# A mixing layer's second product packed from twelve matmuls a block to eleven, with whole token blocks transposed

## The chip, the cores and the metric

The kernel runs on one core of a Trainium2 chip. The metric is the device time of one execution in microseconds, as the median of several runs. A core has TensorE (PE in the profile, its weight loads PEld), VectorE (DVE), ScalarE (ACT), GpSimd (POOL) and SyncE (SP), whose queue (SPq) issues all DMAs of this kernel.

## The reference

x has 2048 tokens of 448 numbers. After a layernorm, a two-dimensional Fourier filter and a mixer work on the same input, and both results are added to x:

```python
x = A_x
xn = _layernorm(x, axis=-1)
return x + _A_ref(xn, A_w_r, A_w_i) + _B_ref(xn, B_w1, B_w2, B_w3, B_w4)
```

The change is in the first half of the mixer:

```python
h = _gelu(_layernorm(x, axis=-1) @ w1)
c = D // 4
g0 = jnp.pad(h[:, :, 0*c:1*c], ((0, 0), (1, 0), (0, 0)))[:, :S, :]   # shift +1
g1 = jnp.pad(h[:, :, 1*c:2*c], ((0, 0), (0, 1), (0, 0)))[:, 1:, :]   # shift -1
g2 = jnp.pad(h[:, :, 2*c:3*c], ((0, 0), (2, 0), (0, 0)))[:, :S, :]   # shift +2
g3 = jnp.pad(h[:, :, 3*c:   ], ((0, 0), (0, 2), (0, 0)))[:, 2:, :]   # shift -2
hs = jnp.concatenate([g0, g1, g2, g3], axis=-1) @ w2
x1 = x + hs
h2 = _gelu(_layernorm(x1, axis=-1) @ w3) @ w4
return x1 + h2
```

So each quarter of h (112 columns) is moved by one or two tokens up or down, and the product with w2 (448 x 448) mixes the quarters. w3 is 448 x 1792, w4 is 1792 x 448.

## The kernel before

**Blocks.** Token a*16 + b stands in partition a of block b, so there are 16 blocks of 128 tokens. A shift by tokens takes a quarter from another block, and only where it wraps around (blocks 0, 1, 14 and 15) does the partition change by one. The blocks are worked in groups of four: 14, 15, 0, 1; then 2 to 5; 6 to 9; 10 to 13.

**Precision.** All large products are in 16 bits with each operand as a high and a low half: high x high, high x low and low x high are added up in PSUM (PASS). ScalarE makes the high half and VectorE or POOL the low one (split_w, and the last operations of w1_unit and ln2). Weights are scaled by a power of two found from the sum of their squares (squares, powers).

**Stages.** warm_up first keeps TensorE busy with matmuls on zeros (line 817). norm1 normalizes a group in place; its refine() on POOL makes the exact scales, among them gsc, which the gelu uses. T1 transposes a group on TensorE (line 374), and the halves go to xT (378, 379). w1_in is the first product (line 414). w1_unit applies the gelu (433), writes the halves of h for one block to a buffer hs of 2 x 4 quarters, each of 112 columns padded to 128 (434, 435), and one DMA transpose of 8 x 128 columns (438) takes it to hT, where the tokens lie along the columns. w2_tile (line 454) makes a block of the second product with 4 quarters x 3 passes = 12 matmuls on 112 rows each, the quarter k taken from the block at distance SHIFT[k], at a column offset for the wrap; it then adds x (456). ln2 is the second layernorm; its transposes (490) go to x2all. turn() transposes the fourth group by DMA (842). front (line 385) and back (line 787) are the products with w3 and w4. Further on come the Fourier stages and the rest of the second mixer product.

**Order.** Each engine works its own queue in order. A scheduler sets the order from the program's priorities and from its own estimates; behind(...) fixes that one operation is issued after another. While TensorE's queue has products of several stages, the pieces of a block of w2_tile can stand between them.

**Memory.** x2mem holds x2all; its later part first holds w4 as it is loaded (w4raw, four loads from line 228, issued behind the transposes of the second and third group), so x2all's groups from the second on have to wait for w4's split.

Of the kernel before, what the change touches and what calls it, by code (L numbers as in the profile page):

```python
# [12 lines left out]
F32 = mybir.dt.float32  # L13
# [7 lines left out]
NB, NC = 16, 16  # L21
# [4 lines left out]
SHIFT = [1, -1, 2, -2]  # L26
WARM = 28
# [9 lines left out]
HS = 3  # L37
# [31 lines left out]
def constants():  # L69
# [20 lines left out]
    for c in range(NC):  # L90
        for j8, (k1, t) in enumerate(slots(c)):
            for j, (kr, s, base) in enumerate(rows(c)):
                if base != k1:
                    continue
                phi = tau * np.outer(np.arange(NB), kr + 128 * np.arange(16)) / S
# [28 lines left out]
def body(tc, nc, x, wf, w1, w2, w3, w4, c_g, c_n, c_small, out):  # L124
# [46 lines left out]

    def stage(name, n, side, dtype=F32):
        t = pw.tile([128, 1808], F32, tag=f"stage{side}", bufs=1, name=name)
        return (t if dtype is F32 else t.bitcast(dtype))[:, :n]
# [19 lines left out]
    def load_x(g):  # L194
        for b0 in sorted(GRP[g])[::2]:
            SY.dma_start(xt[b0 // 2], xv[:, b0:b0 + 2])
# [9 lines left out]
    SY.dma_start(w2s[:112], w2.rearrange("(k p) n -> p k n", p=112))  # L206
# [14 lines left out]
    x2mem = pw.tile([128, 9 * F], F16, name="x2mem")  # L221
    x2all = x2mem[:, 0:8 * F].rearrange("p (j t n) -> p j t n", j=4, t=7)
    w4raw = x2mem.bitcast(F32)[:, F:].rearrange("p (f n) -> p f n", f=14)
    w4v = w4.rearrange("(f p) n -> p f n", p=128)
    W4F = (0, 4, 8, 11, 14)

    def load_w4(i):
        SY.dma_start(w4raw[:, W4F[i]:W4F[i + 1]], w4v[:, W4F[i]:W4F[i + 1]])

    csm = pc.tile([128, 2 * (256 + 2 * DF + 452 + 128)], F16, name="csm")  # L230
# [162 lines left out]
    w2p = pr.tile([112, 2, 4, D], F16, name="w2p")  # L393
# [3 lines left out]

    def h_alloc(g):
        t = {0: 0, 1: 1, 2: 2, 3: 1}[g]
        hT[g] = pr.tile([128, 8, 512 if g else 592], F16, tag=f"h{t}", name=f"h{g}")  # L400
        if g == 0:
            P.memset(hT[g][:, :, 0:576].rearrange("p t (b a) -> p t b a", b=4)[:, :, :, 0:16], 0.0)
            P.memset(hT[g][:, :, 576:592], 0.0)

    def h_at(g, i):
        return 128 * i if g else 144 * i + 16
# [9 lines left out]

    hs_buf = [p1.tile([128, 2, 4, 128], F16, name=f"hs{i}") for i in range(HS)]
    for t in hs_buf:
        P.memset(t.rearrange("p i k n -> p (i k) n")[:, :, 112:], 0.0)

    for o in (0, 1024):
        hs_buf.append(x2mem[:, o:o + 1024].rearrange("p (i k n) -> p i k n", i=2, k=4))
        P.memset(hs_buf[-1].rearrange("p i k n -> p (i k) n")[:, :, 112:], 0.0)

    def w1_unit(g, i, pm=None):
        if pm is None:
# [4 lines left out]
        pv_ = pm.rearrange("p (k n) -> p k n", k=4)  # L431
        h = hs_buf[c % (HS if g == 3 else HS + 2)]
        A.activation(out=pm, in_=pm, func=AF.Gelu_apprx_tanh, scale=gsc[:, c:c + 1])
        u = A.activation(out=h[:, 0, :, 0:112], in_=pv_, func=AF.Copy, scale=h1)
        v = V.scalar_tensor_tensor(out=h[:, 1, :, 0:112], in0=pv_, scalar=h1, in1=h[:, 0, :, 0:112],
                                   op0=ALU.mult, op1=ALU.subtract)
        o = h_at(g, i)
        d = SY.dma_start_transpose(out=hT[g][:, :, o:o + 128], in_=h.rearrange("p i k n -> p (i k n)"))
        after[g, i] = u.ins, v.ins
        after["h", g, i] = (d.ins,)  # L440

    def w2_tile(b):
        pm = bank("sp", f"pw2_{b}")
        n = 0
        for k in (2, 0, 1, 3):
            src, o = b - SHIFT[k], 1
            if src < 0:
                src, o = src + NB, 0
            elif src >= NB:
                src, o = src - NB, 2  # L450
            g, i = WHERE[src]
            o += h_at(g, i) - 1
            for hi, wi in ((0, 0), (0, 1), (1, 0)):
                T.matmul(pm[:, :D], hT[g][:112, 4 * hi + k, o:o + 128], w2p[:, wi, k], start=n == 0, stop=n == 11)  # L454
                n += 1
# [311 lines left out]
    def back(G, fp):  # L767
# [10 lines left out]
        for i in range(2):  # L778
# [12 lines left out]
            if end:  # L791
                with prio(EVAC):
                    for r, to in parts:
                        V.scalar_tensor_tensor(out=xb(b)[:, r], in0=to, scalar=p34[:, min(G, 1):min(G, 1) + 1],  # L794
                                               in1=xb(b)[:, r], op0=ALU.mult, op1=ALU.add)
                        if G > 4:
                            SY.dma_start(ov[:, b, r], xb(b)[:, r])
# [271 lines left out]
```

## Time and profile before

| | |
|---|---|
| median of 3 runs | 410.89 us (410.64 to 411.07) |
| the profiled execution | 410.65 us, span 408.9 us |
| TensorE busy | 402.3 us, 98% of the span |
| VectorE, ScalarE, POOL busy | 330.7, 256.5 and 95.3 us |
| TensorE's granted clock | 1.00 |

A row of the chain of waits or of the timeline begins with its start and its length in us. In a row of groups the number behind x is a count, then come the busy time in us and the mean of one in ns. A row of windows gives for one stretch the busy time of PE, PEld, DVE, ACT and POOL, then the clock, the DMA share and GB/s. A row of DMA issues ends with the median time from issue to landing. L numbers are lines of the kernel.

### The profile page before, as it was taken

What the parts mean: (1) busy time and instruction counts of PE and PEld (TensorE: products, weight loads), DVE (VectorE), ACT (ScalarE), POOL (GpSimd) and SP (SyncE); (2) the same over time, 40 slices, a digit from 0 to 9 for tenths busy, and PEclk for the clock granted to TensorE, in tenths of its full rate; (3) what the DMA queues carried; (4) which work ended last, traced back from release to release, by engine and by line L of the source; (5) the groups of instructions that cost most, each with busy time, mean ns of one, the idle gap of its engine ahead of it and who ended that gap; (6) DMA issues with size and microseconds to landing.
All of it is one profiled execution on the core that took longest, in us unless ns stands there. A gap on an engine that the chain in (4) does not pass through costs nothing.

```text
span 408.9 us, 8745 instructions
## 1 busy us (share of the span) xinstructions
PE 402.3 (98%) x3409; PEld 299.0 (73%) x3409; DVE 330.7 (81%) x686; ACT 256.5 (63%) x434; POOL 95.3 (23%) x172
## 2 busy tenths in 40 slices
PE   7999999999999999999999999999999999999996
PEld 3655555765668777777887887877777779998995
DVE  4888999898857678887798888955899989966645
ACT  4698879973758866556598888863453554453431
POOL 3877720101336748400012111110000000000000
PEclk9999999999999999999999999999999999999999
DMA  8959879914786456516255666500011022100101
GB/s 278 354 192 179 153 149 321 177 62 90 156 231 202 137 196 210 170 59 183 63 145 143 155 156 171 147 27 3 24 68 69 25 88 85 55 2 2 45 2 45
DMA packets 56168, 51.28 MB, mean 125 GB/s; under 512 B 37632, under 2 KB 50496, under 8 KB 56128
## 3 DMA queue, kind: packets, MB, share of 16 engines
q1 hardware_dynamic: 56128, 50.74, 46.0%
q8 instruction: 26, 0.43, 0.4%
q14 instruction: 14, 0.11, 0.1%
HBM read 38.28 MB, written 3.67 MB: 103 GB/s over the span
## 4 chain that ended last, share of the span: by engine, by line
PE 94%; DVE 3%; DMA 2%; POOL 0%; issue 0%; ACT 0%; SPq 0%; POOLq 0%
PE pw L385 33%; PE acc L787 23%; PE pw L454 9%; PE pw L414 6%; PE side L757 4%; PE acc L757 3%; PE pu L646 3%; PE ps L543 3%; PE pe L667 2%; PE pp L601 2%; PE px L618 2%; PE py L688 2%; DVE sta L293 1%; DMA xt<-x 1%; DMA h<-hs 1%; PE pta L374 1%
## 5 line engine op out<-in xcount | busy, mean ns | idle before, releaser
L385 PE MATMUL pw<-x2mem,w3p 128*128 128x256 f16 x1232 | 151.1, 273 | 0.0
L385 PEld LDWEIGHTS <-w3p 128*128 128x128 f16 x1232 | 119.2, 98 | 20.6
L787 PE MATMUL acc<-w4p,hf 128*128 128x448 f16 (+1 forms) x516 | 105.4, 348 | 0.0
L787 PEld LDWEIGHTS <-hf 128*128 128x128 f16 x516 | 49.8, 98 | 36.5
L705 ACT ACTIVATE pw<-pw,pe 128x512 f32<-128x512 f32 x42 | 27.5, 655 | 35.7 <-PE pw L385 35.7
L708 DVE SCALAR_TENSOR_TENSOR hf<-pw,h,hf 128x512 f16<-128x512 f32 x42 | 31.3, 748 | 14.5 <-ACT hf L707 14.4
L454 PE MATMUL pw<-w2p,h 112*128 112x448 f16 x192 | 39.9, 352 | 0.8 <-DMA h<-hs 0.8
L414 PE MATMUL pw<-w1p,xT 128*128 128x448 f16 x176 | 35.4, 352 | 0.0
L627 POOL TENSOR_TENSOR z<-te 128x450 f32<-128x450 f32 x16 | 15.7, 982 | 70.3 <-DVE te L625 70.3
L454 PEld LDWEIGHTS <-h 112*128 112x128 f16 x192 | 18.6, 98 | 17.2 <-DMA h<-hs 1.0
L707 ACT ACTIVATE hf<-pw,h 128x512 f16<-128x512 f32 x42 | 28.7, 686 | 1.0
L414 PEld LDWEIGHTS <-xT 128*128 128x128 f16 x176 | 16.9, 98 | 16.4 <-DVE xT L379 0.8
L723 ACT ACTIVATE hz<-g,h 128x896 f16<-128x896 f32 x14 | 14.6, 1044 | 22.3 <-DVE g L720 22.2
L757 PEld LDWEIGHTS <-hz 128*128 128x128 f16 x294 | 28.2, 98 | 0.4
L608 ACT ACTIVATE pf<-pp 64x450 f16<-64x450 f32 x32 | 17.4, 544 | 12.3 <-DVE pf L609 8.0
L609 DVE TENSOR_TENSOR pf<-pp,pf 64x450 f16<-64x450 f32 x32 | 19.9, 622 | 3.4 <-ACT pf L608 3.0
L724 DVE SCALAR_TENSOR_TENSOR hz<-g,h,hz 128x896 f16<-128x896 f32 x14 | 16.1, 1150 | 7.6 <-ACT hz L723 7.6
L623 ACT ACTIVATE te<-px 64x450 f32<-64x450 f32 x32 | 17.3, 542 | 1.2 <-PE px L618 0.6
L526 POOL TENSOR_TENSOR f<-xr 128x452 f32<-128x452 f32 x16 | 16.4, 1046 | 0.6
L717 ACT ACTIVATE g<-pw,pe 128x512 f32<-128x512 f32 x14 | 9.6, 684 | 10.2 <-PE pw L385 10.1
L794 DVE SCALAR_TENSOR_TENSOR xt<-acc,p,xt 128x448 f32<-128x448 f32 (+1 forms) x17 | 10.9, 654 | 6.2 <-PE acc L787 6.0
L523 POOL TENSOR_TENSOR xr<-xf 128x452 f32<-128x452 f32 x8 | 9.7, 1211 | 26.7 <-issue 20.3
(183 smaller groups left out, 705.7 us busy)
## 6 DMA issues: line engine op xcount, KB each, us to landing
wc<-wf SPq DMA_DIRECT2D x32, 225.0 KB, 3.8
wl<-wf SPq DMA_DIRECT2D x8, 450.0 KB, 4.1
xt<-x SPq DMA_DIRECT2D x8, 448.0 KB, 7.9
xf<-x SPq DMA_DIRECT2D x8, 448.0 KB, 3.6
loads<-x SPq DMA_DIRECT2D x7, 448.0 KB, 4.0
out<-xt SPq DMA_DIRECT2D x13, 224.0 KB, 1.9
w3raw<-w SPq DMA_DIRECT2D x3, 896.0 KB, 12.6
gn<-c_g SPq DMA_DIRECT2D x16, 128.0 KB, 3.1
```

The lines of the kernel that those rows point to most:

```text
L385: T.matmul(ps_out, wp[:, wi + t, cols], xT[:, xi + t, tok], start=t == 0 and wi + xi == 0, stop=t == 3 and wi == 4)
L414: T.matmul(pm[:, :D], xTs[g][:, xi + t, 128 * i:128 * i + 128], w1p[:, wi + t], start=t == 0 and p == 0, stop=t == 3 and p == 2)
L454: T.matmul(pm[:, :D], hT[g][:112, 4 * hi + k, o:o + 128], w2p[:, wi, k], start=n == 0, stop=n == 11)
L526: P.tensor_tensor(out=f[:, :, k:k + 2].rearrange("p b s d -> p s b d"), in0=u[:, :, 0], in1=u[:, :, 1], op=op)
L608: A.activation(out=hi, in_=src, func=AF.Copy)
L609: V.tensor_tensor(out=lo, in0=src, in1=hi, op=ALU.subtract)
L623: A.activation(out=e[64 * h:64 * h + 64], in_=px_[64 - 64 * h:128 - 64 * h, :2 * DF], func=AF.Copy)
L705: A.activation(out=pm, in_=pm, func=AF.Gelu_apprx_tanh, scale=r3)
L707: i = A.activation(out=h[:, 0], in_=pm, func=AF.Copy, scale=h3)
L708: j = V.scalar_tensor_tensor(out=h[:, 1], in0=pm, scalar=h3, in1=h[:, 0], op0=ALU.mult, op1=ALU.subtract)
L757: m = T.matmul(to, h[:, hi, 128 * blk:128 * blk + 128], b[wi], start=new and n == 0, stop=n == 2 and (last if blk in (2, 5, 3, 0) else end ...
L787: m = T.matmul(to, h[:, hi, o:o + 128], w4p[0][:, wi, f, r], start=first and f % 2 == 0 and n == 0, stop=end and f % 2 == 1 and n == 2, sk ...
```

## The change

- **Eleven matmuls a block.** A block's four shifted quarters of h now lie side by side: 448 high halves and 448 low ones, 896 columns, which one DMA transpose turns into seven tiles of 128 rows. w2p has eleven matching weight tiles of 128 rows; tile 3 and the ones behind it hold w2's high half shifted by 64 rows, copied by two DMAs from SBUF to SBUF, and the last is w2's low end with zeros below.
- **Quarters to their places.** w1_unit writes the four quarters of a block directly into the slots of its four neighbour blocks in x2mem (slots_of). The blocks are renumbered (FIRST = 2: block 14 has tokens a*16), and the columns of w1 and rows of w2 are reordered on the way in, so that this is one regular pattern; VectorE writes the low half in two operations. Where the shift wraps, move() shifts two slots by one partition with DMAs of 112 and 15 rows: wrap_on after the first group, wrap_back, with two copies on POOL behind it, before blocks 14 and 15 are transposed. A block is transposed when its last neighbour has been written (DONE).
- **First products block by block.** For the first group, the third and fourth row tile of w1 are worked block by block instead of all blocks by row tile; POOL's refine() of the first group comes behind the split of w1; the gelus of the first two blocks are no longer held behind the second group's transposes.
- **w4 behind w3.** Four of w4's 14 row blocks are loaded after the first part of w3, six after its last part, into a buffer of their own; only the first four go to x2mem later. The sums of squares of w4 move accordingly.
- x's two tiles of the first group change their order of loading; 24 warm-up matmuls instead of 28; less scratch memory for DMAs issued in software.

```diff
-SHIFT = [1, -1, 2, -2]
-WARM = 28
+TURN = [3, 1, 0, 2]
+DONE = {c: [c - 2] for c in range(2, 12)} | {12: [10, 13], 13: [11, 12, 14, 15]}
+FIRST = 2
+WARM = 24
...
-w4raw = x2mem.bitcast(F32)[:, F:].rearrange("p (f n) -> p f n", f=14)
+w4half = [x2mem.bitcast(F32)[:, 2 * F:2 * F + 4 * D].rearrange("p (f n) -> p f n", f=4),
+          p1.tile([128, 10, D], F32, name="w4half")]
...
+load_w4(4, 4)
...
+def slots_of(c, i):
+    t = slot(c - 2)[:, i]
+    return bass.AP(t.tensor, t.offset, [list(t.ap[0]), [3 * 896 + 224, 2], [896 + 112, 2], [1, 112]])
+pairs = [x2mem[:, 896 * b + 3584:896 * b + 5376] for b in (-4, 12, 14)]
+def move(to, frm, by):
+    for o, n in ((0, 112), (112, 15)):
+        SY.dma_start(to[o + (by > 0):o + (by > 0) + n], frm[o + (by < 0):o + (by < 0) + n])
+def wrap_on():
+    move(pairs[1], pairs[0], -1)
+    P.memset(pairs[0][0:1], 0.0)
+    P.memset(pairs[2], 0.0)
+def wrap_back():
+    move(pairs[0], pairs[2], 1)
+    for b, k in ((-2, slice(224, 448)), (-1, slice(336, 448))):
+        P.tensor_copy(out=slot(b)[:, :, k], in_=slot(b - 2)[:, :, k])
...
-    u = A.activation(out=h[:, 0, :, 0:112], in_=pv_, func=AF.Copy, scale=h1)
-    v = V.scalar_tensor_tensor(out=h[:, 1, :, 0:112], in0=pv_, scalar=h1, in1=h[:, 0, :, 0:112],
-                               op0=ALU.mult, op1=ALU.subtract)
-    o = h_at(g, i)
-    d = SY.dma_start_transpose(out=hT[g][:, :, o:o + 128], in_=h.rearrange("p i k n -> p (i k n)"))
+    u = A.activation(out=h[0], in_=pv_, func=AF.Copy, scale=h1)
+    for k in range(2):
+        v = V.scalar_tensor_tensor(out=h[1][:, k], in0=pv_[:, k], scalar=h1, in1=h[0][:, k],
+                                   op0=ALU.mult, op1=ALU.subtract)
+    for b in DONE.get(GRP[g][i], ()):
+        if b == 14:
+            wrap_back()
...
+        d = SY.dma_start_transpose(out=hT[b // 4][:, :, 128 * (b % 4):128 * (b % 4) + 128],
+                                   in_=slot(b if b < 14 else b - 16).rearrange("p i n -> p (i n)"))
...
 def w2_tile(b):
     pm = bank("sp", f"pw2_{b}")
-    for k in (2, 0, 1, 3):
...
-        for hi, wi in ((0, 0), (0, 1), (1, 0)):
-            T.matmul(pm[:, :D], hT[g][:112, 4 * hi + k, o:o + 128], w2p[:, wi, k], start=n == 0, stop=n == 11)
+    h = hT[b // 4][:, :, 128 * (b % 4):128 * (b % 4) + 128]
+    for n, (k, w) in enumerate([(k, w) for k in range(3) for w in (k, k + 7)] + [(3, 10)] + [(k, k) for k in (3, 4, 5, 6)]):
+        T.matmul(pm[:, :D], h[:, k], w2p[:, w], start=n == 0, stop=n == 10)
...
-for t in range(4):
+for t in range(2):
     w1_in(0, list(enumerate(first)), [t])
-n1[0][0]()
+for unit in enumerate(first):
+    w1_in(0, [unit], [2, 3])
+with behind("w1", 3):
+    n1[0][0]()
...
+for k in range(2):
+    w1_unit(0, k, first[k])
 with behind("a1"):
-    w1_unit(0, 0, first[0])
     n1.append(norm1(2, [P, V, A, P]))
 with behind("a1"), behind("n", 2):
-    for k in range(1, 4):
+    for k in range(2, 4):
         w1_unit(0, k, first[k])
+wrap_on()
...
+    SY.dma_start(w2p[64:128, 3:7], w2p[0:64, 0:4])
+    SY.dma_start(w2p[0:64, 4:7], w2p[64:128, 0:3])
...
 with behind("h", 1, 3):
     load_w3([3])
+    load_w4(8, 6)
...
 with behind("t", 3), behind("h", 2, 3), behind("b0"):
-    for i in range(4):
-        load_w4(i)
+    load_w4(0, 4)
```

More of the change, by code (lines that the diff above doesn't have):

```diff
@@ L392, in body @@
     w1p = p1.tile([128, 8, D], F16, name="w1p")
-    w2p = pr.tile([112, 2, 4, D], F16, name="w2p")
+    w2p = pr.tile([128, 11, D], F16, name="w2p")
+    P.memset(w2p[64:128, 10], 0.0)
     hT = {}
[L398 to L406, printed above, removed]
     def w1_in(g, units, ts, passes=range(3)):
@@ L415, in w1_in, with slot @@
                                  start=t == 0 and p == 0, stop=t == 3 and p == 2)
[L417 to L423, printed above, removed]
+    def slot(b):
+        return x2mem[:, 896 * b + 3584:896 * b + 4480].rearrange("p (i n) -> p i n", i=2)
+    def slots_of(c, i):
+        t = slot(c - 2)[:, i]
+        return bass.AP(t.tensor, t.offset, [list(t.ap[0]), [3 * 896 + 224, 2], [896 + 112, 2], [1, 112]])
+    pairs = [x2mem[:, 896 * b + 3584:896 * b + 5376] for b in (-4, 12, 14)]
+    P.memset(pairs[0], 0.0)
+    P.memset(pairs[1][96:128], 0.0)
+    def move(to, frm, by):
[9 more added lines that the diff above has]
+            P.tensor_copy(out=slot(b)[:, :, k], in_=slot(b - 2)[:, :, k])
     def w1_unit(g, i, pm=None):
@@ L430, in w1_unit @@
         pm = pm[:, :D]
[L431 to L432 removed]
+        pv_ = pm.rearrange("p (i j n) -> p i j n", i=2, j=2)
+        h = [slots_of((GRP[g][i] + 2) % NB - 2, k) for k in range(2)]
         A.activation(out=pm, in_=pm, func=AF.Gelu_apprx_tanh, scale=gsc[:, c:c + 1])
[L434 to L436 removed]
@@ L872, in body @@
     with behind("w1", 3):
-        squares(m2[:112], flat(w2s[:112]))
+        squares(m2, flat(w2s))
     T1(1, range(3))
@@ L910, in body @@
             squares(m3[:, k:k + 1], w3raw[:, k])
+    for i in (2, 3):
+        with behind(2, 2):
+            squares(m4[:, i:i + 1], flat(w4raw(2 * i, 2)), junk4)
     s3, r3 = powers(m3, 4, "3", "mm")
```

74 lines of the change are left out of this document (33 added, 41 removed).

## The prediction

> **What bounds the kernel now.** I read the page first: span, busy shares, and the groups of the two kinds of matmul that the change is about.
>
> ```profile
> span 408.9 us, 8745 instructions
> ...
> PE 402.3 (98%) x3409; PEld 299.0 (73%) x3409; DVE 330.7 (81%) x686; ACT 256.5 (63%) x434; POOL 95.3 (23%) x172
> ...
> L454 PE MATMUL pw<-w2p,h 112*128 112x448 f16 x192 | 39.9, 352 | 0.8 <-DMA h<-hs 0.8
> L414 PE MATMUL pw<-w1p,xT 128*128 128x448 f16 x176 | 35.4, 352 | 0.0
> ```
>
> TensorE is busy for 402.3 of 408.9 us: only 6.6 us are holes. So a matmul that is taken away counts in full, unless a hole opens somewhere else. The token-mixing product is L454, 192 matmuls; one on 112 rows is recorded at 352 ns, and L414 on 128 rows at the same 352, so filling up the rows of a matmul costs nothing.
>
> Next the waits of TensorE, and the chain of waits up to the place where both kernels do the same work again.
>
> ```profile
> PE wps L817 <- DVE wsrc L187: 1.2, 1, 1.2
> PE pm L249 <- DVE pt L247: 1.1, 1, 1.1
> PE pw L454 <- DMA h<-hs: 0.8, 1, 0.8
> ```
>
> ```profile
> 9.90 0.38 PE pm L249 x2
> 10.28 1.94 PE pta L374 x16
> 12.23 8.41 PE pw L414 x44
> ...
> 47.10 8.51 PE pw L454 x45
> ```
>
> Before the tail there are three holes, and only the third (0.8 us at 33 us, for the first transposed quarter) belongs to the stage that is changed. From 9.9 us to there TensorE never stands. The last row gives the price of a matmul in a full queue: 8.51 / 45 = 0.189 us. It is this pitch that counts, not the 352 ns, which overlap.
>
> **The change part by part.**
>
> *Eleven instead of twelve.* 16 blocks lose one matmul each: 16 x 0.189 = **-3.0 us**. The moving side keeps 448 columns. All of it lies before 123 us; behind that TensorE's queue holds the same matmuls in the same order in both kernels, so what is won or lost by then stays.
>
> *Start.* x's tokens 0 and 1 are loaded first and 24 instead of 28 warm-up matmuls run. In the built program ScalarE now puts its layernorm of a block ahead of its last sum of squares.
>
> ```profile
> 8.43 0.58 ACT L242 ACTIVATE xr<-w1s 64x448 f16<-64x448 f32 x1
> ...
> 9.00 0.75 ACT L320 ACTIVATE xt<-xt,nma,vy 128x448 f32<-128x448 f32 x1
> ```
>
> VectorE's statistics may start a microsecond earlier, but the scale of w1 waits for these squares: 8.43 + 0.7 + 0.7 gives 9.8, and the small product at 9.90 stays where it is. **0 us** (-0.7 if the squares go first, +0.4 if they come later). POOL clears more memory first: three fills of 1792 columns, estimated at 1.6 us each from the row below, end near 7 us; its first normalization stood at 9.04, so they are hidden up to that.
>
> ```profile
> 1.93 0.52 POOL L402 MEMSET h<- 128x512 f16 x1
> ...
> 9.04 1.16 POOL L323 TENSOR_SCALAR xt<-xt,vy,nma 128x448 f32<-128x448 f32 x1
> 10.17 0.20 POOL L333 TENSOR_TENSOR vq<-vq,va 128x8 f32<-128x8 f32 x1
> ...
> 12.27 0.66 POOL L340 TENSOR_TENSOR vr<-vz,vw 128x8 f32<-128x8 f32 x1
> ...
> 15.66 0.30 POOL L341 TENSOR_SCALAR gsc<-vr,pe 128x4 f32<-128x4 f32 x1
> ...
> 16.07 2.03 POOL L266 TENSOR_TENSOR w1p<-w1s,w1p 128x448 f16<-128x448 f32 x2
> ...
> 19.03 1.18 POOL L323 TENSOR_SCALAR xt<-xt,vy,nma 128x448 f32<-128x448 f32 x1
> ```
>
> *First products block by block.* This step takes something back. POOL's refinement of the first scales (gsc, the scale of the gelu) moves behind the split of w1. ScalarE has w1's third high half at about 14.1 (13.65 and 0.5), so POOL's two low halves (1.0 each, from 2.03) end at 16.2; the refinement is 2.76 us from L333 to the end of L340, 0.2 before and 0.3 behind it: gsc comes at 19.4 instead of 16.0. Behind it, after some 0.5 us of small operations, stands the normalization of block 2, now 19.9 to 21.1 (it ended at 20.2). Block 2 is the first thing that TensorE transposes after the first products, so that starts at 21.1 instead of 20.6, when the first products are done (12.23 + 8.41). Then ScalarE and VectorE (the first row is for the 14.1 above):
>
> ```profile
> 13.05 0.60 ACT L378 ACTIVATE xT<-pta 128x512 f16<-128x512 f32 x1
> ...
> 21.12 2.05 ACT L378 ACTIVATE xT<-pta 128x512 f16<-128x512 f32 x4 [1.51 <-PE pta L374]
> 23.07 2.14 ACT L433 ACTIVATE pw<-pw,gsc 128x448 f32<-128x448 f32 x4
> ```
>
> ```profile
> 23.08 1.40 DVE L379 TENSOR_TENSOR xT<-pta,xT 128x512 f16<-128x512 f32 x2
> ...
> 24.64 2.20 DVE L293 BATCH_NORM_STATS2 sta<-xt 128x6 f32<-128x448 f32 x4
> ...
> 29.62 1.27 DVE L435 SCALAR_TENSOR_TENSOR hs<-pw,h,hs 128x448 f16<-128x448 f32 x2
> ```
>
> In the new queue of ScalarE two gelus and two copies (0.53 each, from 2.14 / 4) are put ahead of or among the four copies out of PSUM, so the last of these ends at 24.2 instead of 23.2. VectorE gets two low halves of h (0.7 each: 0.64 for a whole one, now cut in two) and the small operations of w2's scale ahead of the last low half of xT, which ends at 25.7 instead of 24.5. TensorE can do nine matmuls of the second group first (23.2 to 24.9) and then waits for it. **+1.2 us** at this place. Ends: 0 (in this stretch TensorE had no hole, so it cannot gain) and +2.5, if small operations run twice as long.
>
> *A block's four quarters in one tile.* Before, a block's product could begin with the quarters that were there, and the queue shows it in threes; now a single transpose brings the whole tile, issued when its last neighbour block is done. For block 0, VectorE follows with statistics (2.2), scales, h of block 2, a normalization, and h of blocks 0 and 1: about 6.1 us behind 25.7, 31.8. The transposes:
>
> ```profile
> 39.96 1.22 SPq L216 DMA_DIRECT2D w3raw<-w  x2
> 44.67 1.24 SPq L438 DMA_TRANSPOSE h<-x2mem  x1
> ...
> 61.86 2.55 SPq L228 DMA_DIRECT2D x2mem<-w  x4
> ...
> 73.74 6.62 SPq L438 DMA_TRANSPOSE h<-hs  x4
> ...
> 95.15 13.57 SPq L490 DMA_TRANSPOSE x2mem<-y  x8
> ```
>
> ```profile
> h<-hs SPq DMA_TRANSPOSE x12, 3.2
> ...
> xf<-x SPq DMA_DIRECT2D x8, 448.0 KB, 3.6
> ...
> ...
> x2mem<-w SPq DMA_DIRECT2D x2, 672.0 KB, 10.0
> ```
>
> 31.8 + 3.2 = 35.0. TensorE has 35 matmuls from 25.7 (6.6) and 16 transposes (2.0) to do, 34.3: a hole of 0.7, in place of the old 0.8. **-0.1 us** (-0.8 to +2). Its second half needs w2's copied rows: two copies on SP behind that transpose, issued at about 33.1 and 33.6, with the 3.6 us of the nearest load 37.2; TensorE gets there at 37.2. SP's queue also gets the wrapped quarters, 112 and 15 rows twice. The first pair goes out at about 24 us and is wanted only by blocks 12 and 13. The second pair stands ahead of the transposes of blocks 14 and 15. The last h was ready before the last transpose of the row at 73.74, so at about 79.1; four transposes of 1.24 issued ahead, the copy 3.6, POOL's two small copies about 1, then 3.2 and 1.24 for the transposes: landed near 93. TensorE's queue counts on, with 0.109 for a matmul of 256 columns (72.81 row below), from 47.5 (see the third rival) to the first accumulating matmul: 143 x 0.189 + 92 x 0.109, 84.6; and 59 x 0.189 + 18 x 0.109 more to block 14, 97.7. Behind the waiting SP stand the constants and the second layernorm's transposes from block 4 on, which went out only from 95.15.
>
> ```profile
> 72.81 4.91 PE pw L385 x45
> ```
>
> *w4 behind w3.* Ten blocks of w4 are issued by about 41 us instead of from 61.86 on, and the sums of their squares move ahead of w3's split on ScalarE. That makes w4's scale earlier, which is worth something only if VectorE can use it:
>
> ```profile
> 76.00:81.00 5.00, 5.00 (x41) 3.81 (x40) 3.43 (x10) 5.00 (x11) 0.64 (x1) 1.00 0.76 144
> 81.00:96.00 15.00, 15.00 (x101) 9.70 (x100) 15.00 (x35) 9.42 (x14) 1.03 (x1) 1.00 0.20 53
> ```
>
> ```profile
> 88.53 1.15 DVE L269 SCALAR_TENSOR_TENSOR w4p<-x2mem,pe,w4p 128x896 f16<-128x896 f32 x1
> ```
>
> The third number of a window is VectorE: full for 15 us, and its work grows by 16 x 0.06 = 1 us (h in two parts). It had w4's first blocks at 89.7. In its new queue about 2.6 us less stand ahead of them (87.1), and part of the 1.6 us that it idled from 76 to 81 may go too. TensorE wants their high half at 84.6, which ScalarE makes a microsecond before VectorE's low half, and the low half at 84.6 + 13 matmuls = 87.4. I put **+0.3 us** (0 to +2).
>
> Sum: -3.0 + 0 + 1.2 - 0.1 + 0.3 = **-1.6 us**. The profiled execution took 410.65 us (span 408.9 and 1.75 around it), so 409.05; the median shown is 0.24 above that execution, which makes **409.3 us**.
>
> **The rivals.**
>
> *All of it arrives:* gsc comes in time, the hole of 0.8 closes too: -3.0 - 0.8 from 410.9, 407.1. For it speaks that block 0's chain is no longer than before; against it ScalarE's and VectorE's queues, in which the new work stands ahead.
>
> *VectorE keeps the pace* between 81 and 96 us, and gives TensorE w4's low half no earlier than before, at 89.7: a wait of 2.3 from 87.4 on instead of the 0.3, so +0.4, 411.3. For it the row of 81 to 96; against it the idle time just before that stretch and w4's earlier scale.
>
> *Slower, by w4's early load.* Its last six blocks (1344 KB) and the rest of w3 go out near 40 us, as w3's rest did at 39.96, right ahead of the transpose for block 4 (issued near 45.2; the one for its last neighbour went at 44.67). With 3.2 us that lands at 48.4, and TensorE wants it at 51.6: 35.0 + 66 x 0.189 = 47.5 and 22 more. If it lands like the 672 KB loads (10.0), at 55.2, TensorE stands 3.6 us: +2.0, 412.7. It decides from a landing of 53.2 on. Against it: only four transposes, not eight, share the engines in that stretch.
>
> *The clock* falls in the longer hole behind fewer warm-ups: 4 x 0.216 more, about 2.0 us instead of 1.15.
>
> ```profile
> 1.22 7.53 PE L817 MATMUL wps<-wsrc 128*128 128x512 f16 x28 [1.22 <-DVE wsrc L187]
> ```
>
> 28 matmuls of 512 columns would take 6.0 us at the pitch above (0.216 each); 7.53 shows a slow start that costs 1.5. Once more that cost would make it 410.8. Behind the old hole nothing is slow. [...]
>
> **How the numbers follow.** Forecast 409.3, its own range 408.3 to 410.0: 0.48. All of it 407.1: 0.15. VectorE's pace 411.3: 0.13; the clock 410.8: 0.04. Slower by w4's load or by another late tile, 411.8 to 414: 0.20. About 0.2%, 0.8 us, is what a measurement of this kernel can tell from none. Faster is 0.48 + 0.15 = 0.63, the same 0.17, slower 0.20. For 8 in 10 the range goes from 407.0 to 412.0: it holds the first four cases but for their outer edges.
>
> **What would show it.** L454's successor has 176 matmuls and 33 us in full queue; gsc at 19.4; a hole of TensorE near 21 and 25; one near 34.5 before the first packed product; w2's copies landed by 37; block 4's transpose by 49; no wait of the accumulating matmuls for w4 beyond a microsecond near 85. Wrong would be a wait for a transposed tile that is longer than 2 us, a granted clock below 1 after 10 us, or a stage behind 123 us that is not as long as before.

## The result, and the profile after

The changed kernel takes 413.61 us (median of 10 executions, 412.11 to 414.05) against 410.94 for the kernel before (median of 10): a ratio of 1.0055, 95% interval 1.0041 to 1.0069. It is 2.7 us slower; 409.3 was forecast, and the time lies outside the range. In seven of the ten executions TensorE's granted clock over the whole span is 0.995 or 0.996 and the time 412.9 to 414.05; in three it is 1.000 and the time 412.1 to 412.8. The profiled execution took 414.05 (span 412.2).

First the page of the changed kernel: the span, the busy times, the granted clock by slices, and the two groups of matmuls.

```profile
span 412.2 us, 8724 instructions
...
PE 401.3 (97%) x3389; PEld 298.0 (72%) x3389; DVE 333.9 (81%) x702; ACT 255.8 (62%) x434; POOL 100.9 (24%) x173
...
PEclk9899999999999999999999999999999999999999
...
L415 PE MATMUL pw<-w1p,xT 128*128 128x448 f16 x176 | 35.5, 356 | 1.1 <-DVE xT L389 0.6
L474 PE MATMUL pw<-w2p,h 128*128 128x448 f16 x176 | 35.6, 353 | 0.9 <-DMA h<-x2mem 0.8
```

The packed product does what it should: 176 matmuls instead of 192, 353 ns each. But TensorE is busy only 1.0 us less, although 16 x 0.189 = 3.0 us of product and four warm-ups are gone, and its holes grew from 6.6 to 10.9 us. The 8 in the second slice is a clock that falls (granted 0.50 from 10.9 to 14.3 us). TensorE's order of time (start, length, in brackets the wait ahead of it), changed kernel:

```profile
1.22 6.76 PE L836 MATMUL wps<-wsrc 128*128 128x512 f16 x24 [1.22 <-DVE wsrc L191]
10.19 0.38 PE L259 MATMUL pm<-pt,ones 128*128 128x1 f32 x2 [2.21 <-DVE pt L257]
10.44 3.21 PE L384 MATMUL pta<-ident,xt 128*128 128x128 f32 x16
13.44 8.94 PE L415 MATMUL pw<-w1p,xT 128*128 128x448 f16 x44
...
24.62 1.14 PE L415 MATMUL pw<-w1p,xT 128*128 128x448 f16 x3 [0.32 <-DVE xT L389]
26.05 8.11 PE L415 MATMUL pw<-w1p,xT 128*128 128x448 f16 x41 [0.29 <-DVE xT L389]
34.00 1.91 PE L384 MATMUL pta<-ident,xt 128*128 128x128 f32 x16
...
120.29 2.48 PE L806 MATMUL acc<-w4p,hf 128*128 128x448 f16 x12 [0.69 <-ACT hf L726]
...
132.54 2.56 PE L395 MATMUL pw<-x2mem,w3p 128*128 128x256 f16 x22
...
138.90 0.83 PE L562 MATMUL ps<-csm,xh 128*128 128x128 f16 x12 [0.85 <-DVE y L567]
...
161.65 1.50 PE L562 MATMUL ps<-csm,xh 128*128 128x128 f16 x24 [0.56 <-DVE y L567]
162.99 2.56 PE L395 MATMUL pw<-x2mem,w3p 128*128 128x256 f16 x22
```

The same places in the kernel before:

```profile
10.26 1.97 PE L374 MATMUL pta<-ident,xt 128*128 128x128 f32 x16
12.16 8.48 PE L414 MATMUL pw<-w1p,xT 128*128 128x448 f16 x44
...
31.16 1.04 PE L374 MATMUL pta<-ident,xt 128*128 128x128 f32 x8
...
130.89 2.57 PE L385 MATMUL pw<-x2mem,w3p 128*128 128x256 f16 x22
...
159.61 2.56 PE L385 MATMUL pw<-x2mem,w3p 128*128 128x256 f16 x22
```

Read the two as a running difference. The small product is 0.29 us late, the transposes behind it 0.18. The sixteen transposes behind it are no longer than before in number, yet take 3.21 instead of 1.97, and the first products 8.94 instead of 8.48: 1.70 more. The second group loses another 1.0 (the third group's transposes start at 34.00 against 31.16, of which 0.18 and 1.70 were there already). By 130 us the saved matmuls have brought the difference down to 1.65; and then it rises again, to 3.38 at 160 us, through two waits for y that the kernel before doesn't have.

### The profile page after: what moved, and what is told of

It is laid out like the page before. It is cut to its first block, busy times and chain, and to the rows that moved or that the text cites. A ratio compares the mean times of both kernels' runs of the same rounds, so it can differ in the third digit from the quotient of the medians.

```text
span 412.2 us, 8724 instructions
## 1 busy us (share of the span) xinstructions
PE 401.3 (97%) x3389; PEld 298.0 (72%) x3389; DVE 333.9 (81%) x702; ACT 255.8 (62%) x434; POOL 100.9 (24%) x173
## 4 chain that ended last, share of the span: by engine, by line
PE 60%; DMA 2%; issue 1%; DVE 1%; POOL 0%; SPq 0%
PE pw L395 24%; PE acc L806 16%; PE side L776 4%; PE acc L776 3%; PE pu L665 3%; PE pe L686 2%; PE pp L620 2%; PE px L637 2%; PE py L707 2%; DMA wl<-wf 2%; PE ps L562 1%; DVE wm L270 0%; POOL xr L543 0%; POOL f L545 0%; DVE y L567 0%
## 5 line engine op out<-in xcount | busy, mean ns | idle before, releaser
L806 PEld LDWEIGHTS <-hf 128*128 128x128 f16 x516 | 49.6, 98 | 37.6 <-ACT hf L726 1.0
L474 PE MATMUL pw<-w2p,h 128*128 128x448 f16 x176 | 35.6, 353 | 0.9 <-DMA h<-x2mem 0.8
L474 PEld LDWEIGHTS <-h 128*128 128x128 f16 x176 | 16.9, 98 | 17.1 <-DMA h<-x2mem 2.3
L553 DVE TENSOR_TENSOR xh<-f,xh 128x452 f16<-128x452 f32 x16 | 12.4, 809 | 7.4 <-ACT xh L552 7.4
L545 POOL TENSOR_TENSOR f<-xr 128x452 f32<-128x452 f32 x16 | 17.5, 1116 | 0.6
L690 ACT ACTIVATE e<-pe 128x226 f32<-128x226 f32 x16 | 5.8, 360 | 16.0 <-DVE vh L700 9.0
```

Source lines behind the costliest of these rows:

```text
L474: T.matmul(pm[:, :D], h[:, k], w2p[:, w], start=n == 0, stop=n == 10)
L545: P.tensor_tensor(out=f[:, :, k:k + 2].rearrange("p b s d -> p s b d"), in0=u[:, :, 0], in1=u[:, :, 1], op=op)
L806: m = T.matmul(to, h[:, hi, o:o + 128], w4p[0][:, wi, f, r], start=first and f % 2 == 0 and n == 0, stop=end and f % 2 == 1 and n == 2, sk ...
```

## The experiments

Each experiment gives the median in us, in brackets the lowest and highest execution, then the ratio to the kernel before with its 95% interval. The kernel before, on the same chips, was at 410.9 to 411.0.

**1 and 2: is it the clock?** Experiment 1 gives the changed kernel the 28 warm-up matmuls of before; experiment 2 is the reverse edit in the kernel before.

```
-WARM = 24
+WARM = 28
```

> The changed kernel with 28 warm-up matmuls instead of 24; nothing else is edited, and TensorE's order behind them is the same. Theory (the clock gate): the hole ahead of the first small product was 2.21 us and the first 16 transposes behind it took 3.21 us instead of 1.97; with four more matmuls of 0.216 us the hole is about 1.3 us, the transposes take 2.0 again, the granted clock is 1.000 in every execution, and the time is 1.2 to 1.6 us below that of the changed kernel: 412.0 to 412.4. Rival (the transposes are slow because of what they read or because of the loads beside them): transposes stay at 3.2 us, time 413.6.

> The kernel before with 24 warm-up matmuls instead of 28. Theory (a hole of about 2 us is enough to drop the clock): the hole ahead of the small product goes from 1.15 to 2.0 us, the first transposes take about 3.2 instead of 1.97 us, in most executions, and the time rises by about 1.3 us to 412.2. [...]

Experiment 1: 412.39 (412.2 to 413.4), 1.0039 (1.0027 to 1.0051), clock 1.000 in all five. Experiment 2: 411.65, 1.0017 (1.0004 to 1.0029), in two heaps: six executions at a clock of 0.999 or 1.000 with a median of 410.81, six at 0.995 or 0.996 with 412.48. One fall costs 1.7 us there, and four warm-ups fewer are enough for it in half of the executions. In the changed kernel the seven executions with a fall have a median of 413.72 and the three others 412.28, a difference of 1.4; experiment 1, with no fall, stands at the lower of the two. TensorE's weight loads show how it works; one goes ahead of each matmul (3389 of each in the page above), so that their starts are the matmuls' pace. Changed kernel:

```profile
3.33 0.15 PEld L836 LDWEIGHTS <-wsrc 128*128 128x128 f16 x1 [0.28 <-issue]
3.76 0.15 PEld L836 LDWEIGHTS <-wsrc 128*128 128x128 f16 x1 [0.27 <-issue]
4.15 3.34 PEld L836 LDWEIGHTS <-wsrc 128*128 128x128 f16 x16 [0.24 <-issue]
...
13.81 0.15 PEld L415 LDWEIGHTS <-xT 128*128 128x128 f16 x1 [0.22 <-issue]
14.19 2.83 PEld L415 LDWEIGHTS <-xT 128*128 128x128 f16 x15 [0.22 <-issue]
```

Up to 4.15 us the starts are 0.43 apart, from there on 0.22: the pace doubles (the granted clock is recorded as 1.00 on both sides, so this is read from the pace alone). At 13.8 and 14.2 they are 0.38 apart, twice the pitch of 0.189, and from about 14.3 on the pace is full again. The granted clock of this profile says the same: 0.50 from 11 to 14 us. In the execution of experiment 2 that was profiled the pace came up 3 us later, so the 24 warm-ups lasted longer (8.26 us instead of 6.76), the hole was short (0.53), and nothing fell:

```profile
6.74 0.15 PEld L817 LDWEIGHTS <-wsrc 128*128 128x128 f16 x1 [0.28 <-issue]
7.16 1.83 PEld L817 LDWEIGHTS <-wsrc 128*128 128x128 f16 x9 [0.27 <-issue]
```

```profile
1.22 8.26 PE L817 MATMUL wps<-wsrc 128*128 128x512 f16 x24 [1.22 <-DVE wsrc L187]
10.01 0.38 PE L249 MATMUL pm<-pt,ones 128*128 128x1 f32 x2 [0.53 <-DVE pt L247]
```

So the moment at which the pace comes up helps to decide how long the hole is. The program doesn't fix that moment: the warm-ups begin alike at 1.22 us, and the pace comes up at 4.2 or at 7.2.

**3: the order of the first products**, as before the change:

```
-    for t in range(2):
-        w1_in(0, list(enumerate(first)), [t])
-    for unit in enumerate(first):
-        w1_in(0, [unit], [2, 3])
-    with behind("w1", 3):
-        n1[0][0]()
+    for t in range(4):
+        w1_in(0, list(enumerate(first)), [t])
+    n1[0][0]()
```

(and one gelu instead of two ahead of the third layernorm).

> The changed kernel with the first products in the order of the kernel before: all four blocks by row tile, the refinement of the first scales ahead of them, and one gelu ahead of the third layernorm instead of two. 24 warm-up matmuls stay, so the slow clock stays. Theory (the new order puts gelus ahead of the evacuation of the second group's transposes): the second group's first products no longer wait (0.32 + 0.29 us and the late start of the transposes), about 1.1 us less, 412.5. Rival (what is gained there is given back at the next wait, since the blocks behind are late for another reason): 413.3 to 413.7.

411.18 (410.7 to 412.6), 1.0011 (1.0000 to 1.0023). Again two heaps: seven executions at full clock with a median of 410.93, five at 0.995 or 0.996 with 412.37. At full clock that is 1.46 below experiment 1, and in both heaps it is 1.35 below the changed kernel's (410.93 against 412.28, 412.37 against 413.72). The waits of the second group are gone, and with them those at 120, 139 and 161 us, which I had put down to something else; a new one has come:

```profile
32.98 1.34 PE L384 MATMUL pta<-ident,xt 128*128 128x128 f32 x8 [0.81 <-DVE x2mem L458]
...
37.57 1.31 PE L474 MATMUL pw<-w2p,h 128*128 128x448 f16 x6 [2.15 <-DMA h<-x2mem]
```

Block 0's transposed tile is 2.15 us late as soon as TensorE is early.

**4: w4 loaded late again**, with the sums of its squares in their old order:

```
-    load_w4(4, 4)
...
-        load_w4(8, 6)
...
         load_w4(0, 4)
+        load_w4(4, 4)
+        load_w4(8, 6)
```

> The changed kernel with all of w4 loaded where the kernel before loads it, behind the third group's h, and the sums of squares in the old order. Theory (w4's early load lets the accumulating matmuls of the first expert pair go ahead of the token-mixing products of blocks 12 to 15, whose second layernorm then ends 4 us later, and with it the folds): in the built program the last token-mixing product stands about 6 us earlier in TensorE's queue; the waits at 120 us (0.69 for hf), 139 us (0.85 for y) and 161.7 us (0.56 for y) go: 2.1 us less, 411.5; a wait for w4's low half of up to 1 us may come back near 88 us. Rival (the layernorms are late because GpSimd stands 9.6 us for the second copy of the wrapped quarters): the three waits stay, 413.6.

414.17 (412.44 to 414.71), 1.0070 (1.0055 to 1.0084): not 2 faster but 0.6 slower, and that 0.6 isn't clear of noise, since the interval overlaps that of the changed kernel. The theory falls: the last token-mixing products do stand earlier in TensorE's queue, but the folds (GpSimd's first sums for the Fourier stages, L542) begin hardly earlier (121.60 against 121.85). The rival doesn't hold as written either: in the profile the two waits for y are gone, the one for hf is 1.07, and a wait of 1.41 for h near 76 us has come. So w4's early load isn't what costs the time.

**5: the second copy of the wrapped quarters ahead**, on experiment 1:

```
-        for b in DONE.get(GRP[g][i], ()):
-            if b == 14:
-                wrap_back()
+        if GRP[g][i] == 13:
+            wrap_back()
+        for b in DONE.get(GRP[g][i], ()):
```

> The changed kernel with 28 warm-up matmuls (so that the clock stays up; 412.4 so) and the second copy of the wrapped quarters issued before the transposes of blocks 11 and 12 instead of behind them. TensorE's order is the same. Theory (the wrapped quarters hold up the second layernorm): the memory that the transposed y of blocks 4 to 7 goes into is the memory of the wrapped quarters, so ScalarE waits 7.3 us at 101 us for it, the layernorm of blocks 12 to 15 and the folds run 4 us late, and TensorE waits 0.25 for hf, 0.86 and 0.39 for y behind 118 us. With the copy some 2.6 us earlier these waits shrink to 0.3 in sum or less: 411.0 to 411.4. Rival (the folds are late by the order of VectorE's and ScalarE's queues, not by the copy): the waits stay, 412.4.

411.89 (411.21 to 414.69), 1.0023 (1.0010 to 1.0036): 0.5 below experiment 1, half of what was expected, and the intervals of the two overlap. The rows of the changed kernel that led to it, first GpSimd, then ScalarE, then SyncE:

```profile
91.34 1.50 POOL L445 COPY x2mem<-x2mem 128x448 f16<-128x448 f16 x2 [9.64 <-DMA x2mem<-x2mem]
```

```profile
101.59 0.67 ACT L495 ACTIVATE y<-xt,nm 128x448 f32<-128x448 f32 x1 [7.32 <-DMA x2mem<-y]
```

```profile
85.90 2.23 SPq L435 DMA_DIRECT2D x2mem<-x2mem  x2
91.96 2.60 SPq L466 DMA_TRANSPOSE h<-x2mem  x2
94.62 0.57 SPq L961 DMA_DIRECT2D csm<-c_small  x1
96.39 17.90 SPq L509 DMA_TRANSPOSE x2mem<-y  x8
```

SyncE issues the copy at 85.90, and what stands behind it (the tiles of blocks 14 and 15, the constants, the transposes of the second layernorm's y) waits until GpSimd has added its part at 92; ScalarE then stands 7.3 us for a buffer that these transposes empty. No matmul waits there. What comes of it shows 20 us later, in the folds, whose first one starts at 121.85 in the changed kernel and at 117.57 in the kernel before. The profiled execution of experiment 5 is the one of twelve that started 1.1 us late (414.69), and its clock falls like the changed kernel's; in it the waits for hf and the first one for y are gone, that near 162 is 0.88, and a new one of 1.07 for h stands near 90. Its folds begin at 121.81, so measured from the late start they are 1.1 us earlier than in the changed kernel.

The copy isn't the whole cause, though. In experiment 3 it keeps its place in SyncE's queue; it is issued there at 83.41, the transposes of y from 93.99 on, the folds begin at 117.72, and no wait is left behind 100 us. With the old order, moving the copy no longer makes the folds earlier: 117.48 in experiment 9 without the move, 117.88 in experiment 12 with it. In these profiles the copy holds something up only where the stages ahead of it are late already.

**6 and 7: both together, and w2's copies in another queue.** Experiment 6 is 3 with 28 warm-ups. Experiment 7 adds:

```
-        SY.dma_start(w2p[64:128, 3:7], w2p[0:64, 0:4])
-        SY.dma_start(w2p[0:64, 4:7], w2p[64:128, 0:3])
+        A.dma_start(w2p[64:128, 3:7], w2p[0:64, 0:4])
+        A.dma_start(w2p[0:64, 4:7], w2p[64:128, 0:3])
```

> The changed kernel with the old order of the first products and 28 warm-up matmuls. Theory (the clock and the order are two separate losses, 1.7 us in some executions and 1.4 in all): granted clock 1.000 in every execution and the time of the fast half of the run with the old order alone, 410.9 (410.7 to 411.1). Rival (the two overlap, the longer warm-up pushes the start): 411.5 or more.

> As the run with the old order and 28 warm-up matmuls, but the two copies of w2's rows are issued from ScalarE's queue instead of SyncE's, where they stand ahead of the first transposes of h. Theory (block 0's transposed tile is late, a hole of TensorE of 2.15 us at 35.4 us, because SyncE stands for w2's copies until 33.8): the transposes go out about 1 us earlier, the hole shrinks to about 1.1, 409.9 to 410.2. Rival (the hole is set by VectorE's low half of the last quarter, or ScalarE pays for the issue): 410.7 to 411.2.

Both expectations fail. Experiment 6: 412.45 (412.17 to 412.60), 1.0033 (1.0021 to 1.0045), the clock at 0.995 or 0.996 in all five. It didn't fall at the start but behind block 0's hole:

```profile
37.79 0.39 PEld L474 LDWEIGHTS <-h 128*128 128x128 f16 x3 [2.69 <-DMA h<-x2mem]
38.40 0.15 PEld L474 LDWEIGHTS <-h 128*128 128x128 f16 x1 [0.22 <-issue]
...
41.01 0.15 PEld L415 LDWEIGHTS <-xT 128*128 128x128 f16 x1 [0.22 <-issue]
41.38 1.04 PEld L474 LDWEIGHTS <-h 128*128 128x128 f16 x6 [0.22 <-issue]
```

0.37 apart from 38.0 to 41.4. Experiment 3 had nearly the same hole (35.4 to 37.57) and no fall in its profiled execution. Experiment 7 took 416.06 (1.0123, 1.0110 to 1.0136): the first transpose went out at 32.55 instead of 33.99, as meant, but TensorE still got its tile only at 37.6. It waits 3.40 us for it, since no first product stands ahead of it any more, and the slow pace lasts longer than in experiment 6, to 42.1 us instead of 41.4; the granted clock over the span is 0.992 in this profile and 0.995 in that one (last section).

```profile
DMA to landing us min/median/max: 2.9/3.1/5.0
```

The slowest transpose of h took 5.0 us there, 3.1 is the median. It is one of the first four, and if it is the first, 32.55 and 5.0 make 37.55, the end of TensorE's wait. So it isn't only the issue that is late. That the copies in flight at the time (wrapped quarters and w2) hold the transpose up is what this suggests; experiment 9 takes one of them away.

**8: twelve matmuls again**, on experiment 6, one of them made twice (so the output counts that product double):

```
-        for n, (k, w) in enumerate([(k, w) for k in range(3) for w in (k, k + 7)] + [(3, 10)] + [(k, k) for k in (3, 4, 5, 6)]):
-            T.matmul(pm[:, :D], h[:, k], w2p[:, w], start=n == 0, stop=n == 10)
+        for n, (k, w) in enumerate([(k, w) for k in range(3) for w in (k, k + 7)] + [(3, 10)] * 2 + [(k, k) for k in (3, 4, 5, 6)]):
+            T.matmul(pm[:, :D], h[:, k], w2p[:, w], start=n == 0, stop=n == 11)
```

> As the run with the old order and 28 warm-up matmuls, but one of the eleven matmuls of each token-mixing product is made twice, twelve a block as before the change (its product counts twice in the output). Theory (a matmul in a full queue costs its pitch): 16 times 0.189 is 3.0 us more, 413.9. Rival (part of the saving only lengthens holes, block 0's of 2.15 us among them, since what TensorE waits for is not made by TensorE): 1.5 to 2.5 us more.

424.93 (1.0333, 1.0320 to 1.0346). It doesn't measure what it was made for: the scheduler turned the queues so that TensorE waits 6.34 us at 74 us for the second layernorm, and the 47 matmuls of 256 columns behind it take 8.16 us, 0.17 each instead of 0.11; the granted clock over the span is 0.984 to 0.988. Experiment 11 replaces it.

**9 and 10: what stands ahead of block 0's transpose.** On experiment 6, first the wrapped quarters' first copy goes behind the four transposes:

```
     for k in range(4):
         w1_unit(1, k)
+    with behind("h", 1, 3):
+        wrap_on()
```

Then (10) w2's copies leave their old place and go behind the first transpose too, and the second wrapped copy goes ahead as in 5:

```
     for k in range(4):
         w1_unit(1, k)
+        if k == 0:
+            with behind("na", 2), behind("h", 1, 0):
+                SY.dma_start(w2p[64:128, 3:7], w2p[0:64, 0:4])
+                SY.dma_start(w2p[0:64, 4:7], w2p[64:128, 0:3])
```

> As the run with the old order and 28 warm-up matmuls (412.45, in which TensorE waited 2.25 us at 35.5 for block 0's transposed tile and the clock fell behind that wait), but the first copy of the wrapped quarters is issued behind the first four transposes of h instead of ahead of them. w2's copies still stand ahead. Theory (SyncE's and the DMA queues' work ahead of the first transpose is what makes block 0's tile late): the transposes go out at 33.0 instead of 34.0 at the earliest and land by 36.5, the hole shrinks to 1.0 to 1.3 us, too short for the clock to fall: 409.7 to 410.2. Rival (the tile is late by VectorE's low half): hole still 2 us, clock still falls, 412.4.

> As the run before, and w2's two copies are issued behind the first transpose of h too, and the second copy of the wrapped quarters ahead of the transposes of blocks 11 and 12. Theory (as before): block 0's first transpose goes out when its last quarter is ready, about 32.0 to 32.5, lands by 35.6, and TensorE, which gets there at 35.4, stands 0.3 us at most; w2's copies land at 37.3 and TensorE may stand 0.5 for them. Clock 1.000, 408.6 to 409.4, faster than both kernels. Rival (the time saved there is lost at the next late tile): 410.5 or more.

Experiment 9: 411.42 (410.37 to 412.99), 1.0014 (1.0001 to 1.0028). The hole shrinks from 2.25 to 0.94, as expected, and the clock fell in one of twelve. The time is 1.0 below experiment 6, but 1.2 above the upper end of what was expected; three executions at full clock lie at 412.8 to 413.0, for which I have no profile. Experiment 10: 411.71 (1.0017, 1.0009 to 1.0026): TensorE waits 1.01 for block 0's tile, 0.45 more in the same block, and 0.92 for a later tile. The clock fell in two of eleven. What is saved at one tile is lost at the next.

**11: the price of a matmul**, in the kernel before. The last product of the fourth quarter is left out, so the output lacks it:

```
-            for hi, wi in ((0, 0), (0, 1), (1, 0)):
+            for hi, wi in ((0, 0), (0, 1), (1, 0))[:3 - (k == 3)]:
```

> The kernel before with eleven instead of twelve matmuls a block: the last of the three products of the fourth quarter is left out, so that part of the token-mixing product is missing from the output. All else is as before, its own transposes and loads. Theory (a matmul in a full queue costs its pitch, 0.189): 16 of them are 3.0 us, 411.0 becomes 408.0 (407.8 to 408.3). Rival (TensorE only gets earlier to what it waits for): 409 or more, with new waits for h, y or hf.

408.71 (408.38 to 409.19), 0.9944 (0.9932 to 0.9957): 2.3 us (1.8 to 2.8 by the interval), not 3.0. Part of the rest shows as new holes, the same kinds as in the changed kernel, and here there is no wrapped copy at all:

```profile
113.44 2.07 PE L787 MATMUL acc<-w4p,hf 128*128 128x448 f16 x10 [0.23 <-DVE hf L708]
134.20 0.83 PE L543 MATMUL ps<-csm,xh 128*128 128x128 f16 x12 [0.27 <-DVE y L548]
```

**12: all that helped**: 28 warm-ups, the old order, both wrapped copies moved (5 and 9).

> The changed kernel with 28 warm-up matmuls, the old order of the first products, the first copy of the wrapped quarters behind the first four transposes of h, and the second copy ahead of the transposes of blocks 11 and 12: all that helped in the runs so far (block 0's hole 0.9 instead of 2.25 us; the second layernorm earlier, worth 0.5). Theory (the losses are separate and add): 0.3 to 0.6 us below the run with the first copy behind, 410.8 to 411.1, which is the time of the kernel before; a gain over it isn't expected, since eleven matmuls alone were worth 2.3 us on the kernel before and block 0's holes, the start and the late layernorm take back 2. Rival (the second layernorm is no longer late once the first products have their old order, so the earlier copy gives nothing): 411.4.

410.8 (410.18 to 414.11), 1.0005 (0.9987 to 1.0022), as expected the time of the kernel before. The waits behind 100 us are gone; what is left are three waits, for a bank of PSUM and for two tiles:

```profile
33.12 1.34 PE L384 MATMUL pta<-ident,xt 128*128 128x128 f32 x8 [0.81 <-DVE x2mem L458]
36.49 1.31 PE L474 MATMUL pw<-w2p,h 128*128 128x448 f16 x6 [0.92 <-DMA h<-x2mem]
53.60 2.25 PE L474 MATMUL pw<-w2p,h 128*128 128x448 f16 x11 [1.05 <-DMA h<-x2mem]
```

**13 and 14: w4's last six blocks away from block 4's tile**, on experiment 12: they move to the place of the first four (13), or directly behind block 4's transpose (14; the second diff).

```
-        load_w4(8, 6)
...
         load_w4(0, 4)
+        load_w4(8, 6)
```

```
-        load_w4(8, 6)
...
     for k in range(4):
         w1_unit(2, k)
+    with behind("h", 2, 0):
+        load_w4(8, 6)
```

> As the run with both copies of the wrapped quarters moved (410.8), but w4's last six blocks (1344 KB) are loaded with its first four, behind the third group's h, instead of behind w3 near 41.5. Theory (the prediction's third rival, in small: the load delays block 4's transposed tile, for which TensorE waited 1.05 us at 52.5): that wait goes, w4's scale is still in time, 409.7 to 410.0, below the kernel before. Rival (the tile is late by SyncE's order or VectorE, and the later load brings a wait for w4 near 88): 410.8 or more.

> As the run before, with w4's last six blocks loaded directly behind the transpose of block 4, near 50 us. Theory: block 4's tile lands as early as without the load, but the tiles of block 3 to 6 and the transposed x of the last group share the DMA queues with it and may be up to 1 us late instead: 409.8 to 410.8. Rival (what counts is that the load is away from the transposes altogether): 1 us more than the run before.

Experiment 13: 411.14 (410.61 to 411.63), 1.0004 (0.9995 to 1.0012). The wait at 53 us is gone, which suggests that the load delayed that tile; but experiment 9, with the load in the same place as 12, waited only 0.22 there, so how much of the 1.05 is the load's isn't shown. 0.89 for h near 84 and 0.33 for y near 159 come in its place, and the time is no lower. Experiment 14: 414.97 (1.0101, 1.0086 to 1.0117), beyond its range and its rival's: behind the load the remaining transposes of x took 7.28 us to issue instead of 3.92, and later waits add up to 4.9 us.

```profile
58.07 4.14 PE L415 MATMUL pw<-w1p,xT 128*128 128x448 f16 x21 [1.40 <-DMA xT<-x]
...
120.62 0.93 PE L806 MATMUL acc<-w4p,hf 128*128 128x448 f16 x4 [1.01 <-ACT hf L726]
...
162.39 1.50 PE L562 MATMUL ps<-csm,xh 128*128 128x128 f16 x24 [1.77 <-DVE y L567]
```

No version that computes the whole layer is faster than the kernel before.

## Why the prediction was wrong, point by point

The forecast was 4.3 us too low. Two steps put a loss at nothing: the clock (0 in the sum, a chance of 0.04), and "what is won or lost by then stays" (no loss behind 123 us). A third, the -3.0 for the matmuls, was too large. What each cost in its place:

- **Eleven instead of twelve, -3.0.** The direction was right and the size too large: 2.3 us on the kernel before (experiment 11). "A matmul that is taken away counts in full, unless a hole opens somewhere else": holes open. The two that experiment 11 shows, 0.23 and 0.27, end with work of VectorE, and make 0.5 of the missing 0.7; the rest isn't located.
- **Start, 0.** 0.29 late by the profile, inside the bound of +0.4. The fills of memory on GpSimd were hidden: the last ends at 7.2 us, its first normalization starts at 8.06.
- **The clock, a rival with a chance of 0.04.** This is the step that failed first. Its mechanism and size were right (1.5 written, 1.4 to 1.7 measured; hole 2.0 written, 2.21 measured); that such a hole leaves the clock alone (the 0 in the sum, the low chance) was assumed, and no row and no run shows it as a rule: the only length that the trace had shown to be harmless was 1.15 us. What the runs show in their place is a fall in 7 of 10 executions, in the profiled one to 0.50 for 3.4 us behind the hole of 2.21; without it the median is 1.2 us lower (experiment 1).
- **First products block by block, +1.2.** Right in its mechanism, and nearly in size: the second group loses 1.0 in the changed kernel. The marks fit too: the scale of the first gelus came at 19.63 (19.4 written), VectorE's last low half of xT in experiment 1 at 25.83 (25.7 written), and two waits stand in the second group. The 1.46 between experiments 1 and 3 lies near the forecast partly by luck, since with the order the waits behind 118 us go too and block 0's longer wait comes.

```profile
19.08 0.55 POOL L351 TENSOR_SCALAR gsc<-vr,pe 128x4 f32<-128x4 f32 x1
```

- **A block's four quarters in one tile, -0.1.** The hole of 0.7 that was written is 0.15 in the changed kernel and 0.89 in experiment 1, where the clock doesn't fall. It stays that short only because the loss above hides the tile: with the order undone TensorE waits 2.15 us, a little beyond the bound of +2. There the first transpose goes out at 33.88 instead of the 31.8 of the prediction, behind the first wrapped copy and w2's copies.
- **w4 behind w3, +0.3.** Better than written: no wait for w4 near 85 us, and late loading is no faster (experiment 4). The rival of a late tile behind the 1344 KB may be the 1.05 us of experiment 12, but isn't what made the kernel slower. Two slips in this part change nothing: 84.6 and 13 matmuls make 87.1, not 87.4, and that rival's sum is 412.9, not 412.7.
- **"What is won or lost by then stays."** Wrong. TensorE's queue is the same behind 123 us, but not the state of the other engines: a delay ahead of 100 us comes back there as waits, 0.69 + 0.85 + 0.56 = 2.1 us. One path is shown: the second wrapped copy was followed as far as TensorE's own wait for blocks 14 and 15 (none, as written) and not through SyncE's queue to the layernorm and the folds. Moving it gives 0.5 by the medians (experiment 5); with the old order all three waits vanish with the copy unmoved (experiment 3), and in experiment 7, where TensorE stands 3.40 us at 34 us, two of them (0.29 and 0.83) are back in spite of the old order. How the 2.1 divides between the copy and the delays ahead of it stays open.

The sum for the profiled execution, from the rows above: -3.0 for the matmuls, +0.2 at the start, +1.7 for the clock, +1.0 in the second group, +2.1 behind 118 us makes +2.0 of the 3.3 by which its span is longer. The rest is in part short waits for h and x (0.15 to 0.41 each), less the 0.79 that the kernel before waits for h, and what a wait hides ahead of it: 3 matmuls in the row at 24.62 take 1.14, where three in a full queue read 0.74 (kernel before, at 36.70), so a recorded wait understates its price. I haven't split that rest further. Left open too is why some executions at full clock are 1 to 2 us above the others (experiments 1, 9 and 12).

## What to carry to other kernels

A matmul saved in a full queue need not be worth its whole pitch: here, with VectorE busy for 81% of the span, 2.3 us of 3.0 arrived (experiment 11). A copy that waits in the queue that issues all transfers has to be followed through everything behind it to the last consumer, also where the matrix engine itself never waits for it. And a warm-up is sized against the moment at which the real work begins: shortening it by 0.9 us cost 1.2 on the median.

## What the runs showed of the hardware that I had not expected

The pace of the warm-ups doubles at another moment in each profile, though they begin alike at 1.22 us. The starts of the weight loads are 0.43 apart up to 3.8 us in the kernel before, 4.2 in the changed kernel, 4.6 in experiments 4, 5 and 7, 5.4 in 1 and 9, 5.8 in 3 and 7.2 in 2 and 6; behind that they are 0.22 apart. The row for experiment 6:

```profile
7.17 2.73 PEld L836 LDWEIGHTS <-wsrc 128*128 128x128 f16 x13 [0.28 <-issue]
```

A fall lasts for some microseconds. In the changed kernel the granted clock is 0.50 from 10.93 to 14.34 us, 3.41 us; half of that, 1.7 us, is an estimate of what it costs, beside the 1.70 that the rows of the first group lose and the 1.4 and 1.7 between the two heaps of executions (changed kernel and experiment 2). In experiment 6 the starts are 0.37 apart from 38.0 to 41.4, in experiment 7 from 38.0 to 42.1:

```profile
42.09 0.14 PEld L474 LDWEIGHTS <-h 128*128 128x128 f16 x1 [0.22 <-issue]
42.33 1.23 PEld L415 LDWEIGHTS <-xT 128*128 128x128 f16 x7
```

The profiles have such a fall behind a hole of 1.73 us in experiment 4, 2.19 in experiment 5, 2.21 in the changed kernel, 2.25 in experiment 6 and 3.40 in experiment 7. The shortest of these, where the sixteen transposes behind the hole take 2.48 instead of 1.97:

```profile
9.98 0.38 PE L258 MATMUL pm<-pt,ones 128*128 128x1 f32 x2 [1.73 <-DVE pt L256]
10.23 2.48 PE L383 MATMUL pta<-ident,xt 128*128 128x128 f32 x16
```

The pace stayed up behind 1.15 us in the kernel before, behind 1.23 and 2.15 in experiment 3 and behind 1.77 near 162 us in experiment 14 (the granted clock over the span is 1.00 in all three). Experiment 4 itself has a harmless hole of 1.41 us, behind which eleven matmuls take 2.25 us, as in a full queue:

```profile
75.80 2.25 PE L473 MATMUL pw<-w2p,h 128*128 128x448 f16 x11 [1.41 <-DMA h<-x2mem]
```

So the length of a hole alone doesn't tell whether the clock falls: behind 1.73 us it did, behind 1.77 and 2.15 it didn't. What else decides isn't shown. Executions of one kernel differ in it too: there is a fall in 7 of 10 of the changed kernel, in 6 of 12 of experiment 2 and in 5 of 12 of experiment 3.
